# Second product of a two-layer network: two of its three partial products take bfloat16 operands

## The chip, the cores and the metric

The kernel runs on one core of one Trainium2 chip. The metric is the device time of one execution in microseconds (us). The kernel before was timed three times: median 1087.86 us, from 1087.34 to 1088.19.

## The reference, cut to what matters

```python
# attention with exponential features: 8 batches x 8 heads, 576 tokens, 64 wide, 128 features
def phi(x):
    proj = x @ w_phi
    proj = proj - max(abs(proj), axis=-1)
    return concatenate([exp(proj), exp(-proj)])
kv, z = phi(k).T @ v, sum(phi(k), tokens)
x = (phi(q) @ kv) / (phi(q) @ z + 1e-06)     # gathered to [4608 tokens, 512]

# then the two-layer network
h = x @ w_in                                  # 512 -> 2048
g = maximum(h, 0.0) ** 2
out = g @ w_out                               # 2048 -> 512
```

All inputs and outputs are float32.

## The kernel before, in words

The program has two parts that run interleaved. The attention part works on 32 pairs of heads (four pairs make a batch). It writes its result, split into two float16 arrays (a rounded value and the rest), into a ring buffer in SBUF that holds 1536 tokens. The network part reads that ring.

The network part cuts the 4608 tokens into 18 chunks of 256 and the 2048 hidden columns into 8 slices of 256. Function `moe(c, f, ...)` handles one chunk and one slice, so there are 144 steps. One step is:

1. `gemm1` (TensorE, line 934) forms the hidden slice in a PSUM tile `ph` of 128 x 512 words. `w_in` and the ring are both kept as two float16 parts, and three of the four part products are formed: 24 matmuls, each with 128 x 128 weights and 256 moving columns.
2. ScalarE takes the relu with a scale (line 943, tile `r`), squares it into `gh` (line 945), rounded to float32r, and squares it again at full precision into PSUM (line 952; in the first 16 steps VectorE does that instead).
3. VectorE subtracts (helper at line 288): `gl` is the exact square less `gh`, and is written as float32r, a four-byte word like `gh`.
4. `gemm2` (TensorE, line 962) adds the slice's share to two output tiles `po` in PSUM, one for each 128 tokens (`i`), 512 columns each. `w_out` is kept as `wout[f][0]` (rounded to float32r) and `wout[f][1]` (the rest, also in float32r). For each `i` and each 128 hidden columns (`j`) it multiplies `gh` by `wout[f][0]`, `gh` by `wout[f][1]` and `gl` by `wout[f][0]`: 12 matmuls of 512 moving columns. The activations are the stationary operand, the weights the moving one.
5. After slice 7 of a chunk, VectorE scales `po` into the tile `o` (line 973), of which there is one buffer, and SyncE's queue stores it (line 976). This is done for `i` = 0 and then for `i` = 1.

The order of instructions on each engine is fixed when the program is built. Every piece of work is registered with an engine, a duration, what it needs and which buffers it uses (`P.add`). A list scheduler (`order`) simulates the engines by these durations. `improve` repeats that 400 times, moves the ranks of a twentieth of the early pieces at random each time, and keeps the shortest plan. So a changed duration of one kind of work can give another order everywhere, in the start of the program too, where SyncE's loads, the attention of the first pairs and the preparation of the weights compete.

Of the kernel before, what the change touches and what calls it, by code (L numbers as in the profile page):

```python
# [15 lines left out]
F32R = mybir.dt.float32r  # L16
F16 = mybir.dt.float16
BF16 = mybir.dt.bfloat16
# [17 lines left out]
T = 256  # L36
# [217 lines left out]
def act_us(n, pointers=0):  # L254
    return 0.2 + n / 1200 + 0.09 * pointers
# [19 lines left out]
def tile_kernel(ctx, tc, qp, kp, vp, w_phi, w_in, w_out, out):  # L275
    nc = tc.nc
    V, A, G, PE, SP = nc.vector, nc.scalar, nc.gpsimd, nc.tensor, nc.sync
    P = Plan()
# [3 lines left out]
    mp = ctx.enter_context(tc.tile_pool(name="moe", bufs=1))  # L282
# [4 lines left out]
    def sub(eng, out_, a, b_):  # L287
        eng.tensor_tensor(out=out_, in0=a, in1=b_, op=ALU.subtract)  # L288

    def tiles(pool, tag, shape, dtype, bufs, first=0):  # L290
        return Tiles(P, pool, tag, shape, dtype, bufs, first)
# [8 lines left out]
    wout = [None] * NFP  # L300
# [43 lines left out]
    po_ = tiles(ps, "po", [128, DM], F32, 2)  # L344

    r_ = tiles(mp, "r", [128, 2, T], F32, 2)
    gh_ = tiles(mp, "gh", [128, 2, T], F32R, 3)
    gl_ = tiles(mp, "gl", [128, 2, T], F32R, 3)
    o_ = tiles(mp, "o", [128, DM], F32, 1)

    dq = cp.tile([32, 2, 32], F32, name="dq")
# [564 lines left out]
    def moe(c, f, w_done):  # L916
        n = c * NFP + f
        m, bank = LEAD + n, n + 2 * BANKS
        half, c0 = divmod(c * T % RING, HR)
        po = [("po", 2 * BANKS + 2 * c + i) for i in range(2)]  # L920

        after = list(w_done[f, True])
        if f == 0:
            for p in range(NPAIR):
                after += [o for t0, t1, o in ring_of[p] if t0 < c * T + T and t1 > c * T]

        def gemm1():
            ph = ph_[bank]
            for j in range(2):
                ff = 2 * f + j  # L930
                k = 0
                for t in range(KT):
                    for (w, x) in ((0, 0), (0, 1), (1, 0)):
                        PE.matmul(out=ph[:, j, :], lhsT=win[w][:, t, 128 * ff:128 * ff + 128],  # L934
                                  rhs=ring[half][x][:, t, c0:c0 + T], start=k == 0, stop=k == 3 * KT - 1)
                        k += 1

        g1 = P.add("PE", 2.58, gemm1, after, [("ph", bank)], m)
        if f:
            g1.after.append(chunk_done[c][-1])  # L940
        chunk_done.setdefault(c, []).append(g1)
        Q = m - 1000.0
        o = P.add("ACT", act_us(512, 1), lambda: A.activation(  # L943
            out=r_[n], in_=ph_[bank], func=AF.Relu, scale=cw[:, f, 0:1]), [g1], [("ph", bank), ("r", n)], Q)
        sq = P.add("ACT", act_us(512), lambda: A.activation(out=gh_[n], in_=r_[n], func=AF.Square),  # L945
                   [o], [("r", n), ("gh", n)], Q)
        if n < WITH_DVE:
            o = P.add("DVE", 0.76, lambda: V.scalar_tensor_tensor(
                out=ph_[bank], in0=ph_[bank], scalar=cw[:, f, 0:1], in1=r_[n], op0=ALU.mult, op1=ALU.mult),
                [o], [("ph", bank), ("r", n)], Q)  # L950
        else:
            o = P.add("ACT", act_us(512), lambda: A.activation(out=ph_[bank], in_=r_[n], func=AF.Square),  # L952
                      [sq], [("ph", bank), ("r", n)], Q)
        o = P.add("DVE", 0.70, lambda: sub(V, gl_[n], ph_[bank], gh_[n].bitcast(F32)),
                  [o, sq], [("ph", bank), ("gh", n), ("gl", n)], Q)

        def gemm2():
            for i in range(2):
                for j in range(2):
                    ff = 2 * f + j  # L960
                    for s, (g, w) in enumerate(((gh_, 0), (gh_, 1), (gl_, 0))):
                        PE.matmul(out=po_[po[i][1]], lhsT=g[n][:, j, 128 * i:128 * i + 128], rhs=wout[f][w][:, j, :],  # L962
                                  start=(ff == 0 and s == 0), stop=(ff == 2 * NFP - 1 and s == 2))

        g2 = P.add("PE", 2.86, gemm2, [o] + list(w_done[f, False]),
                   [("gh", n), ("gl", n)] + po, m + 1.5)
        if f:
            g2.after.append(last2[0])
        last2[0] = g2
        if f == NFP - 1:  # L970
            for i in range(2):
                tt = 2 * c + i
                o = P.add("DVE", 0.8, lambda tt=tt, i=i: V.tensor_scalar(
                    out=o_[tt], in0=po_[po[i][1]], scalar1=cc[:, tt:tt + 1], scalar2=cc[:, tt:tt + 1],
                    op0=ALU.mult, op1=ALU.mult), [g2], [po[i], ("o", tt)], Q)
                P.add("SP", 0.1, lambda tt=tt: SP.dma_start(out[128 * tt:128 * tt + 128, :], o_[tt]),
                      [o], [("o", tt)], Q, land=2.5)
# [5 lines left out]
    w_done = {}  # L983
# [33 lines left out]
    for c in range(NCH):  # L1017
        for f in range(NFP):
            moe(c, f, w_done)
# [37 lines left out]
```

## Time and profile before

| what | value |
|---|---|
| time, median of 3 runs | 1087.86 us |
| time of the profiled execution | 1087.31 us |
| its span, first to last instruction | 1085.5 us |
| TensorE matmuls (PE) | 1063.7 us busy, 98% of the span, 7882 matmuls |
| TensorE weight loads (PEld) | 826.3 us busy, 76% |
| VectorE (DVE) | 737.3 us busy, 68% |
| ScalarE (ACT) | 632.9 us busy, 58% |
| GpSimd (POOL) | 185.6 us busy, 17% |
| mean granted TensorE clock | 0.997 of full speed |

The profile is of one execution. Matmuls are pipelined, so the busy time of one matmul in it (390 ns, say) is longer than the distance to the next one. What a matmul costs in a dense stretch is read from the distance between starts, or from the chain of waits, which gives the length of whole blocks of matmuls. In that chain "PE po L962 x12" is one `gemm2` and "PE ph L934 x24" one `gemm1`.

### The profile page before, as it was taken

The numbers are of one execution on the slowest core, as the hardware profiler recorded it, in microseconds if no ns is written. First come the engines' busy times: TensorE is split into PE (matmuls) and PEld (weight loads), VectorE is DVE, ScalarE is ACT, GpSimd is POOL, SyncE is SP. The second block draws the span as 40 slices with busy tenths as digits, with TensorE's granted clock in tenths as the row PEclk, the third lists the DMA queues.
The fourth block names the chain that finished last, engine by engine and source line by source line (L and its number), as shares of the span: only waits on it lengthen the run. The fifth ranks groups of instructions, "written<-read, shape, count | busy, mean of one in ns | idle before, by whom it ended". The sixth has DMA issues, their size and how long they took to land.

```text
span 1085.5 us, 19971 instructions
## 1 busy us (share of the span) xinstructions
PE 1063.7 (98%) x7882; PEld 826.3 (76%) x7882; DVE 737.3 (68%) x1537; ACT 632.9 (58%) x1125; POOL 185.6 (17%) x87
## 2 busy tenths in 40 slices
PE   7889999999999999999999999999999999999997
PEld 6656777777777777777777777877777777888886
DVE  4589989787778877877878776776777855112111
ACT  6889864466566665656556655665555645333232
POOL 1366531111111111111111111111100111000000
PEclk9999999999999999999999999999999999999999
DMA  8844412212212122222222111112120101000000
GB/s 304 309 126 117 149 46 68 59 35 56 85 45 85 46 75 55 69 62 57 74 56 75 55 60 38 54 55 75 43 63 22 50 14 41 1 21 20 1 20 20
DMA packets 68288, 73.49 MB, mean 68 GB/s; under 512 B 36836, under 2 KB 41828, under 8 KB 68196
## 3 DMA queue, kind: packets, MB, share of 16 engines
q1 hardware_dynamic: 68196, 72.23, 21.8%
q8 instruction: 62, 1.02, 0.4%
q14 instruction: 30, 0.25, 0.1%
HBM read 59.18 MB, written 12.99 MB: 66 GB/s over the span
## 4 chain that ended last, share of the span: by engine, by line
PE 88%; DVE 4%; ACT 3%; DMA 2%; issue 1%; POOL 1%; SPq 0%; DVEq 0%; POOLq 0%
PE po L962 35%; PE ph L934 33%; PE pv L568 4%; PE pp L512 3%; PE pn L786 3%; PE pp L855 3%; PE pv L786 2%; PE pv L573 1%; PE pp L665 1%; PE pn L518 1%; DVE u L415 1%; DMA k<-in_kp_dram 1%; DMA den<-sx 1%; ACT u L412 1%; POOL u L426 1%
## 5 line engine op out<-in xcount | busy, mean ns | idle before, releaser
L934 PE MATMUL ph<-ring,win 128*128 128x256 f16 x3456 | 399.4, 273 | 0.1
L934 PEld LDWEIGHTS <-win 128*128 128x128 f16 x3456 | 328.2, 98 | 67.9 <-issue 30.2
L962 PE MATMUL po<-wout,gh 128*128 128x512 f32 x1152 | 369.6, 402 | 0.0
L962 PEld LDWEIGHTS po<-wout,gh 128*128 128x128 f32 x1152 | 206.8, 189 | 47.8 <-issue 5.6
L943 ACT ACTIVATE r<-ph,cw 128x512 f32<-128x512 f32 x144 | 98.8, 686 | 234.1 <-PE ph L934 233.9
L962 PE MATMUL po<-wout,gl 128*128 128x512 f32 x576 | 226.3, 393 | 0.0
L868 POOL PARTITION_ALL_REDUCE mx<-pt x52 | 113.6, 2184 | 634.3 <-ACT pt L862 528.3
L288 DVE TENSOR_TENSOR gl<-ph,gh 128x512 fp32r<-128x512 f32 x144 | 98.7, 686 | 166.1 <-ACT ph L952 163.5
L962 PEld LDWEIGHTS po<-wout,gl 128*128 128x128 f32 x576 | 108.1, 188 | 25.1 <-DVE gl L288 0.5
L945 ACT ACTIVATE gh<-r 128x512 fp32r<-128x512 f32 x144 | 90.9, 631 | 4.6
L952 ACT ACTIVATE ph<-r 128x512 f32<-128x512 f32 x128 | 74.7, 583 | 0.0
L808 ACT ACTIVATE n<-pn 128x320 f32<-128x320 f32 x26 | 11.4, 438 | 102.4 <-PE pn L786 102.4
L568 PE MATMUL pv<-e,v 128*64 128x256 f32 x512 | 60.9, 380 | 0.4 <-ACT kz L615 0.4
L882 DVE SCALAR_TENSOR_TENSOR pt<-qe,zc,pt 128x576 f32<-128x576 f32 x52 | 42.2, 813 | 22.4 <-ACT pt L880 21.4
L288 DVE TENSOR_TENSOR qe<-pt,mx 128x576 f32<-128x576 f32 x52 | 39.2, 754 | 22.6 <-POOL mx L868 22.3
L534 ACT ACTIVATE e<-e 128x512 f32<-128x512 f32 x64 | 39.8, 621 | 21.4 <-DVE e L531 21.2
L568 PEld LDWEIGHTS pv<-e,v 128*64 128x64 f32 x512 | 35.5, 137 | 15.1 <-ACT kz L615 0.5
L873 ACT ACTIVATE qe<-qe 128x576 f32<-128x576 f32 x52 | 35.0, 673 | 17.2 <-DVE qe L288 17.1
L819 DVE STREAM_TRANSPOSE kvs<-pv 128x256 f32<-128x256 f32 x26 | 11.6, 445 | 47.7 <-PE pv L786 44.4
L880 ACT ACTIVATE pt<-qe,zc 128x576 f32<-128x576 f32 x52 | 39.6, 771 | 3.3
L886 DVE STREAM_TRANSPOSE yt<-pt 128x576 f32<-128x576 f32 x52 | 40.4, 776 | 1.3
L536 ACT ACTIVATE e<-e 128x512 f32<-128x512 f32 x64 | 40.2, 629 | 1.7
(196 smaller groups left out, 1296.0 us busy)
## 6 DMA issues: line engine op xcount, KB each, us to landing
v<-in_vp_dram SPq DMA_DIRECT2D x32, 320.0 KB
k<-in_kp_dram SPq DMA_DIRECT2D x32, 288.0 KB
q<-in_qp_dram SPq DMA_DIRECT2D x32, 288.0 KB
rb<-rd SPq DMA_DIRECT2D x64, 144.0 KB
out_dram<-o SPq DMA_DIRECT2D x36, 256.0 KB
td<-kvs SPq DMA_DIRECT2D x26, 128.0 KB
kz<-td SPq DMA_DIRECT2D x208, 16.0 KB
raw0i<-in_w_in_dram SPq DMA_DIRECT2D x1, 1024.0 KB
```

The lines of the kernel that those rows point to most:

```text
L288: eng.tensor_tensor(out=out_, in0=a, in1=b_, op=ALU.subtract)
L536: exps[p].append(P.add("ACT", act_us(512), lambda n=n: A.activation(out=e_[n][:, :, 0, :], in_=e_[n][:, :, 0, :], func=AF.Exp), [o], [("e" ...
L568: PE.matmul(out=to[64 * h:64 * h + 64, 0:256], lhsT=v_[p][:, t, h, :], rhs=e_[2 * p + h][:, t].rearrange("p s f -> p (s f)"), start=t == 0 ...
L786: PE.matmul(out=to[64 * h:64 * h + 64, :], lhsT=kz_[n][:, 128 * s_ + 64 * h:128 * s_ + 64 * h + 64], rhs=qe_[2 * n + h].rearrange("p (s x) ...
L868: o = P.add("POOL", par_us(S), lambda n=n, h=h: G.partition_all_reduce(mx_[n], pt_[p][:, h, :], channels=128, reduce_op=bass_isa.ReduceOp. ...
L882: o = P.add("DVE", dve_us(S), lambda h=h, qe=qe, y=y: V.scalar_tensor_tensor(out=y(), in0=qe(1), scalar=zc_[p][:, 2 * h + 1:2 * h + 2], in ...
L886: o = P.add("DVE", dve_us(S), lambda n=n, y=y: V.transpose(yt_["y", n - 2 * EARLY], y()), [o], [("pt", p), ("yt", ("y", n - 2 * EARLY))], ...
L934: PE.matmul(out=ph[:, j, :], lhsT=win[w][:, t, 128 * ff:128 * ff + 128], rhs=ring[half][x][:, t, c0:c0 + T], start=k == 0, stop=k == 3 * K ...
L943: o = P.add("ACT", act_us(512, 1), lambda: A.activation(out=r_[n], in_=ph_[bank], func=AF.Relu, scale=cw[:, f, 0:1]), [g1], [("ph", bank), ...
L945: sq = P.add("ACT", act_us(512), lambda: A.activation(out=gh_[n], in_=r_[n], func=AF.Square), [o], [("r", n), ("gh", n)], Q)
L952: o = P.add("ACT", act_us(512), lambda: A.activation(out=ph_[bank], in_=r_[n], func=AF.Square), [sq], [("ph", bank), ("r", n)], Q)
L962: PE.matmul(out=po_[po[i][1]], lhsT=g[n][:, j, 128 * i:128 * i + 128], rhs=wout[f][w][:, j, :], start=(ff == 0 and s == 0), stop=(ff == 2 ...
```

## The change

`gl` becomes a bfloat16 tile. Two of the three partial products in `gemm2` take bfloat16 operands: the product of `gh` and the rest of the weights, and the product of `gl` and the rounded weights. Where a float32r tile is an operand there, only the upper two bytes of each word are read, through a bfloat16 view with a step of two elements. This is so for the stationary `gh` in the second product and for the moving weights in both. The stationary `gl` is contiguous. The product of `gh` and `wout[f][0]` stays in float32r. The loop over the three products becomes the outermost one, and the duration that the scheduler is told for a `gemm2` goes from 2.86 to 2.72.

```diff
-    gl_ = tiles(mp, "gl", [128, 2, T], F32R, 3)
+    gl_ = tiles(mp, "gl", [128, 2, T], BF16, 3)
...
         def gemm2():
-            for i in range(2):
-                for j in range(2):
-                    ff = 2 * f + j
-                    for s, (g, w) in enumerate(((gh_, 0), (gh_, 1), (gl_, 0))):
-                        PE.matmul(out=po_[po[i][1]], lhsT=g[n][:, j, 128 * i:128 * i + 128], rhs=wout[f][w][:, j, :],
+            upper = lambda x: x.bitcast(BF16).rearrange("p j (c w) -> p j c w", w=2)[:, :, :, 1]
+            for s, (g, w) in enumerate(((gh_[n], wout[f][0]), (upper(gh_[n]), upper(wout[f][1])),
+                                        (gl_[n], upper(wout[f][0])))):
+                for i in range(2):
+                    for j in range(2):
+                        ff = 2 * f + j
+                        PE.matmul(out=po_[po[i][1]], lhsT=g[:, j, 128 * i:128 * i + 128], rhs=w[:, j, :],
                                   start=(ff == 0 and s == 0), stop=(ff == 2 * NFP - 1 and s == 2))

-        g2 = P.add("PE", 2.86, gemm2, [o] + list(w_done[f, False]),
+        g2 = P.add("PE", 2.72, gemm2, [o] + list(w_done[f, False]),
```

The order of instructions moves in the whole program. Two places of it matter below. The first is TensorE at the very end, the last `gemm2` of the program (`po_11598` is the output tile of `i` = 0, `po_11605` and in the changed kernel `po_11601` that of `i` = 1; `gh_11846` and `gl_11849` are its activations). Before:

```order
L962 MATMUL po_11598<-wout_1731,gh_11846 128x512 x2
L962 MATMUL po_11598<-wout_1731,gl_11849 128x512
L962 MATMUL po_11598<-wout_1731,gh_11846 128x512 x2
L962 MATMUL po_11598<-wout_1731,gl_11849 128x512
L962 MATMUL po_11605<-wout_1731,gh_11846 128x512 x2
L962 MATMUL po_11605<-wout_1731,gl_11849 128x512
```

And in the changed kernel:

```order
L965 MATMUL po_11598<-wout_1659,gh_11846 128x512 x2
L965 MATMUL po_11601<-wout_1659,gh_11846 128x512 x2
L965 LDWEIGHTS gh_11846
L965 MATMUL po_11598<-wout_1659,gh_11846 128x512
...
L965 LDWEIGHTS gl_11849
L965 MATMUL po_11598<-wout_1659,gl_11849 128x512
L965 LDWEIGHTS gl_11849
L965 MATMUL po_11598<-wout_1659,gl_11849 128x512
L965 LDWEIGHTS gl_11849
L965 MATMUL po_11601<-wout_1659,gl_11849 128x512
```

Before, the tile of `i` = 0 had all its shares after six of the twelve matmuls; now it has them after ten. A bfloat16 matmul has a weight load of its own in the program, as the float16 ones of `gemm1` have; a float32r matmul is one instruction that loads its own weights.

The second place is the queue of loads on SyncE at the start of the program (`k`, `q` and `v` are a pair's inputs, `raw0i` and `raw1i` the first two slices of `w_in`; the difference, with - for before and + for the changed kernel):

```order
 L504 DMA k_116<-in_kp_dram 128x576
 L505 DMA q_118<-in_qp_dram 128x576
 L469 DMA v_120<-in_vp_dram 128x640
+L403 DMA raw1i<-in_w_in_dram 128x4x512
+L504 DMA k_158<-in_kp_dram 128x576
+L505 DMA q_162<-in_qp_dram 128x576
+L469 DMA v_167<-in_vp_dram 128x640
 L403 DMA raw0i<-in_w_in_dram 128x4x512
-L469 DMA v_149<-in_vp_dram 128x640
-L504 DMA k_159<-in_kp_dram 128x576
-L505 DMA q_164<-in_qp_dram 128x576
```

One slice of `w_in` stands ahead of the second pair's keys in both, the other slice now and `raw0i` before; the second pair's `v` is now behind its keys and queries.

## Prediction

> **What bounds the kernel now.** I read the page's first and fourth parts first, then busy time by stretches, then who waited for whom.
>
> ```profile
> span 1085.5 us, 19971 instructions
> PE 1063.7 (98%) x7882; PEld 826.3 (76%) x7882; DVE 737.3 (68%) x1537; ACT 632.9 (58%) x1125; POOL 185.6 (17%) x87
> PE 88%; DVE 4%; ACT 3%; DMA 2%; issue 1%; POOL 1%; SPq 0%; DVEq 0%; POOLq 0%
> PE po L962 35%; PE ph L934 33%; PE pv L568 4%; PE pp L512 3%; PE pn L786 3%; PE pp L855 3%; PE pv L786 2%; PE pv L573 1%; PE pp L665 1%; PE pn L518 1%; DVE u L415 1%; DMA k<-in_kp_dram 1%; DMA den<-sx 1%; ACT u L412 1%; POOL u L426 1%
> 0.00:120.00 120.00, 104.24 (x1054) 73.59 (x1055) 87.20 (x142) 100.86 (x168) 54.10 (x28) 0.99 0.60 205
> 120.00:1080.00 960.00, 959.42 (x6831) 752.71 (x6828) 649.33 (x1395) 532.04 (x958) 131.51 (x59) 1.00 0.18 50
> PE pn L375 <- DVE et L541: 0.3, 1, 0.3
> ```
>
> The last three are the two stretches (length, then busy us of PE, PEld, DVE, ACT, POOL, then granted clock) and the whole list of TensorE's waits after 120 us: one wait, 0.3 us. From 120 to 1080 us TensorE is busy 959.42 of 960 us at clock 1.00. So a nanosecond taken off a matmul there comes off the end, and `gemm2` is 35% of the chain. TensorE idles only at the start, 120 − 104.24 = 15.8 us, and after its last matmul.
>
> What a matmul costs is read from the chain of waits in a dense late stretch (start, length, block) and from the groups:
>
> ```profile
> 950.45 2.76 PE po L962 x12
> 953.21 5.26 PE ph L934 x48
> 958.47 5.48 PE po L962 x24
> L934 PE MATMUL ph<-ring,win 128*128 128x256 f16 x3456 | 399.4, 273 | 0.1
> L934 PEld LDWEIGHTS <-win 128*128 128x128 f16 x3456 | 328.2, 98 | 67.9 <-issue 30.2
> L962 PE MATMUL po<-wout,gh 128*128 128x512 f32 x1152 | 369.6, 402 | 0.0
> L962 PEld LDWEIGHTS po<-wout,gh 128*128 128x128 f32 x1152 | 206.8, 189 | 47.8 <-issue 5.6
> L962 PE MATMUL po<-wout,gl 128*128 128x512 f32 x576 | 226.3, 393 | 0.0
> ```
>
> A float32r matmul of 512 columns takes 2.76 / 12 = 230 ns (228 in the block of 24). A float16 one of 256 columns takes 5.26 / 48 = 109.6 ns; two of them, 512 columns, take 219 ns. So columns of two-byte operands already go by at a higher rate here, with their weight load (98 ns) under the 109.6 ns. The 189 ns load of a float32r matmul lies under 230 ns.
>
> **The change part by part.**
>
> *Eight of twelve matmuls, in 144 steps: 1152 matmuls.* Each took 230 ns. A contiguous two-byte matmul of 512 columns isn't in the trace. It is bounded above by the two halves, 219 ns, since these hold whatever fixed part a matmul has twice. The fixed part is at most what the 109.6 ns leave beside the 98 ns load, some 11 ns, so the lower bound is 219 − 11 = 208 ns. I take 216, a fixed part of 3 ns, nearer to the upper bound because nothing suggests that a load sets the pace at 256 columns. The saving is 14 ns each (11 to 22), so 1152 × 14 ns = 16.1 us (12.7 to 25.3).
>
> [...]
>
> *The step of two.* No two-byte operand with a step is in the trace. The nearest row for the moving side is the float32r matmul itself: a step of two over two-byte elements passes over the same 2 KB per partition and product as the 512 four-byte words, which go by in 230 ns. So the memory delivers those bytes at least at that rate, and the bound above is no gain at all (230, the first rival). Below it is the contiguous 216. I take 216: in the profile nothing separates bytes passed over from bytes used. On the stationary side (`gh`, 576 loads) the bounds are the 98 ns and 189 ns loads. Either fits under a 216 ns matmul.
>
> [...]
>
> *The change of type within a step.* After a float32r matmul, the next float16 load isn't drawn under it:
>
> ```profile
> 952.82 0.39 PE L962 MATMUL po<-wout,gl 128*128 128x512 f32 x1
> 953.05 5.42 PE L934 MATMUL ph<-ring,win 128*128 128x256 f16 x48
> 953.05 0.44 PEld L934 LDWEIGHTS <-win 128*128 128x128 f16 x5 [0.26 <-issue]
> ```
>
> The loads stand idle 0.26 us until the float32r matmul has run its 0.23 us. The cost is small: the 48 that follow keep to 109.6 ns on average. This switch moves from the end of `gemm2` to its middle, and the one from two-byte to four-byte operands stays at the start. I take 0. If the strided load that now stands there were slow, 189 − 98 = 91 ns more in each step would be uncovered, 144 × 91 ns = 13.1 us (second rival).
>
> *What stays.* 576 float32r matmuls at 230 ns. VectorE's subtraction writes two bytes instead of four:
>
> ```profile
> L288 DVE TENSOR_TENSOR gl<-ph,gh x144: 640/691/694, 106.8 to 1076.4; 128x512 fp32r<-128x512 f32 x144
>   PEld po L962: 0.5, 1
>   PEld L934: 0.4, 1
> ```
>
> The last two rows are TensorE's only waits for it, 0.9 us in all. `gl` is now needed at the ninth matmul, not the third, some 1.3 us later. Its cover is the steps between `gemm1` and `gemm2` in TensorE's order: 0, even if the subtraction's 691 ns should change either way by a third (0.23 us).
>
> *The end.* The last `gemm2`, VectorE's scaling and the stores (SPq: SyncE's queue):
>
> ```profile
> 1077.07 0.62 PE L962 MATMUL po<-wout,gh 128*128 128x512 f32 x2
> 1078.63 0.81 DVE L973 TENSOR_SCALAR o<-po,cc 128x512 f32<-128x512 f32 x1 [1.56 <-PE po L962]
> 1079.47 3.30 SPq L976 DMA_DIRECT2D out_dram<-o  x2
> 1079.57 0.39 PE L962 MATMUL po<-wout,gl 128*128 128x512 f32 x1
> 1081.60 0.81 DVE L973 TENSOR_SCALAR o<-po,cc 128x512 f32<-128x512 f32 x1 [2.16 <-DMA out_dram<-o]
> ```
>
> The second scaling at 1081.60 waits for the first store, because `o` has one buffer, and not for TensorE, which started its last matmul 2 us earlier. So the end hangs on the moment when the tile of `i` = 0 is complete. That was after 6 matmuls, 6 × 0.230 = 1.38 us from the block's start; now it is after ten, 4 × 0.230 + 6 × 0.216 = 2.22 us. That adds 0.8 us. The other tile is complete two matmuls later and still waits for the store. At the other 17 chunk ends TensorE has `gemm1` blocks to do: 0 there.
>
> *The order.* The scheduler's other order changes the start. Of the 15.8 us idle before 120 us, the wait for the first keys stays:
>
> ```profile
> PE po L512 <- DMA k<-in_kp_dram: 4.9, 2, 4.6
> ```
>
> The other 11 us hang on which of many short waits come last. In both orders a slice of `w_in` precedes the second pair's keys. I have no row for the new order and take 0, within ±3 us (a quarter of what is open).
>
> **Sum:** 1087.31 (the profiled execution) − 16.1 + 0.8 = 1072.0 us. The median before lies 0.55 above that execution, so I predict 1072.5 us. The likeliest case's own range is 1062 to 1079: the saving's bounds and ±3 for the start.
>
> **Rivals.**
>
> 1. *A strided word costs what a float32r word costs.* If the 14 ns come from passing 2 KB per partition through the port, they stay, as all eight matmuls have a strided moving operand. For it: the only matmuls here with four bytes per column are the ones at 230. Against it: nothing in the rows, for there is no second length of float32r to tell a fixed part from a rate. Time: 1087.86 + 0.8 = 1088.7, within ±3.
> 2. *The late load is slow.* In each step the strided load after the last float32r matmul stands open for 91 ns more: 1072.5 + 13.1 = 1085.6. If it isn't overlapped with the next load either, 2 × 13.1 brings 1098.7. For it: the 0.26 us gap shows that this load isn't drawn forward. Against: the five loads after the gap, 98 ns each, end within 0.44 us, less than 5 × 98 = 490 ns, so one of them ran beside another.
> 3. *Slower: the moving port halves its rate at a step of two*, two reads where one served. Place: every one of the 1152. Price: 432 ns instead of 216, so 1152 × (432 − 230) ns = 232.7 us, 1321 us. It decides as soon as a strided column costs over 6.5% (14 of 216 ns) more than a contiguous one: then the gain is gone and every further per cent is 2.5 us of loss. For it: no such operand has a row. Against: a four-byte column already takes only 230.
> 4. *The new start loses what TensorE wins.* It would take twice the 11 us that are open there. Little speaks for it.
>
> **How the numbers follow.** The forecast gets 0.76, rival 1 0.10, rival 2 0.07, rival 3 0.03, rival 4 and the rest 0.04. A measurement of this kernel can tell about 0.2% (2.2 us) from no change. Faster than 1085.7 is the forecast whole, half of rival 2 and a part of the rest: 0.81. Within 0.2%: most of rival 1 at 1086 to 1090 and a part of rival 2: 0.09. Slower: rival 3, the long form of rival 2, the upper part of rival 1: 0.10. The range is 1064 to 1085.6: it holds nearly all of the forecast's own and the short form of rival 2, and leaves out 2 in 10.
>
> **What would show it.** In the changed profile a whole `gemm2` should be 4 × 230 + 8 × 216 = 2.65 us in the chain of waits (2.76 before), and its bfloat16 loads should take 98 ns. 2.76 would be rival 1. A gap of over 0.1 us between the fourth and the sixth matmul of a block would be rival 2. A block over 4 us would be rival 3. After 120 us TensorE should still wait for almost nothing, and its idle time before 120 us should be 13 to 19 us. The second scaling at the end should start about 2.97 us after the first, and that 2.2 us into the last block. The forecast is wrong if the blocks are shorter but TensorE waits in the middle, or if bfloat16 with a step keeps 230.

## The result and the profile after

The changed kernel takes 1095.68 us (median of 14 runs, 1093.43 to 1097.23), the kernel before 1087.78 us in the same comparison. The ratio is 1.0064, with a 95% interval from 1.005 to 1.0078: slower, by 7.9 us, where 1072.5 us was forecast. The profiled execution took 1096.09 us.

The page of the changed kernel: its span, the busy time, the granted clock in 40 slices, and the groups of the second product.

```profile
span 1094.3 us, 19959 instructions
PE 1065.5 (97%) x7882; PEld 719.7 (66%) x7882; DVE 739.7 (68%) x1537; ACT 634.6 (58%) x1125; POOL 181.6 (17%) x87
PEclk9898899999999999999999999999999999999999
L965 PE MATMUL po<-wout,gl 128*128 128x512 bf16 x576 | 153.2, 387 | 0.0
L965 PEld LDWEIGHTS <-gl 128*128 128x128 bf16 x576 | 55.1, 96 | 74.7
L965 PEld LDWEIGHTS <-gh 128*128 128x128 bf16 x576 | 44.5, 98 | 76.3 <-issue 39.3
```

The kernel does what the change says (the clock's row is read further down): all 1152 matmuls are bfloat16 and their weight loads take 96 to 98 ns instead of 188. Two things differ from the forecast. The first is the length of a block in the chain of waits (start, length, block):

```profile
953.71 2.75 PE po L965 x12
961.82 5.24 PE ph L934 x48
967.06 5.49 PE po L965 x24
```

A `gemm2` takes 2.75 us. It was 2.76 before and was forecast at 2.65. The second is the start. Here are the first 120 us as a whole, then cut in two places (length, busy us of PE, PEld, DVE, ACT and POOL, granted clock, share and rate of the DMAs), and TensorE's longest waits:

```profile
0.00:120.00 120.00, 98.82 (x972) 67.62 (x973) 83.88 (x137) 98.11 (x162) 47.19 (x27) 0.90 0.60 205
...
40.00:60.00 20.00, 15.46 (x157) 10.61 (x158) 10.40 (x22) 13.83 (x26) 6.33 (x4) 0.83 0.54 184
100.00:120.00 20.00, 15.78 (x130) 9.17 (x130) 17.28 (x23) 17.88 (x28) 11.65 (x6) 0.74 0.41 124
...
PE pp L656 <- ACT qe L674: 5.7, 3, 4.5
PE pn L518 <- DMA k<-in_kp_dram: 4.2, 1, 4.2
PE po L512 <- DMA k<-in_kp_dram: 2.3, 1, 2.3
```

By 120 us TensorE has finished 972 matmuls, against 1054 before, and its clock is granted at 0.90, against 0.99. In the clock's row above, the slices with an 8 are the second, the fourth and the fifth, all within the first 137 us. The network part starts later. This is the group of the relu, which every step has once (duration, then first and last start), before and after:

```profile
L943 ACT ACTIVATE r<-ph,cw x144: 662/687/700, 103.5 to 1074.5; 128x512 f32<-128x512 f32 x144
```

```profile
L943 ACT ACTIVATE r<-ph,cw x144: 666/688/706, 123.9 to 1082.5; 128x512 f32<-128x512 f32 x144
```

The 8.8 us between the two profiled spans (1085.5 and 1094.3) fall into three parts, by the times in the traces. The 21st relu starts at 251.0 us before and at 263.3 us after: 12.3 us lost. From there to the last relu it takes 823.5 us before and 819.3 after: 4.2 us won. From the last relu to the end it takes 11.0 and 11.7 us: 0.7 us lost. (These times, and others to the nanosecond below, are starts read from the traces at full resolution.)

The end is as forecast. The last block, the scalings and the stores of the changed kernel:

```profile
1087.59 0.81 DVE L976 TENSOR_SCALAR o<-po,cc 128x512 f32<-128x512 f32 x1 [2.48 <-PE po L965]
1088.42 3.29 SPq L979 DMA_DIRECT2D out_dram<-o  x2
1090.55 0.81 DVE L976 TENSOR_SCALAR o<-po,cc 128x512 f32<-128x512 f32 x1 [2.15 <-DMA out_dram<-o]
```

The first scaling starts 5.1 us after the last relu (1082.5), 4.1 us before.

So two questions had to be settled: why the bfloat16 matmuls won so little, and whether the start lost its time through the order of instructions.

### The profile page after: what moved, and what is told of

It reads as the page before. It is cut to its first block, busy times and chain, and to the rows that moved or that the text cites. A ratio compares the mean times of both kernels' runs of the same rounds, so it can differ in the third digit from the quotient of the medians.

```text
span 1094.3 us, 19959 instructions
## 1 busy us (share of the span) xinstructions
PE 1065.5 (97%) x7882; PEld 719.7 (66%) x7882; DVE 739.7 (68%) x1537; ACT 634.6 (58%) x1125; POOL 181.6 (17%) x87
## 4 chain that ended last, share of the span: by engine, by line
PE 91%; ACT 2%; DVE 1%; DMA 1%; issue 1%; DVEq 0%; ACTq 0%
PE po L965 37%; PE ph L934 35%; PE pv L568 4%; PE pp L512 3%; PE pn L786 3%; PE pp L855 2%; PE pv L786 2%; PE pv L573 1%; PE pp L665 1%; PE pn L518 1%; DMA raw5o<-in_w_out_dram 0%; PE pn L682 0%; ACT u L412 0%; PE pp L656 0%; DVE u L415 0%
## 5 line engine op out<-in xcount | busy, mean ns | idle before, releaser
L934 PEld LDWEIGHTS <-win 128*128 128x128 f16 x3456 | 335.8, 98 | 72.4 <-issue 6.4
L965 PE MATMUL po<-wout,gh 128*128 128x512 f32 (+1 forms) x1152 | 302.9, 404 | 0.0
L288 DVE TENSOR_TENSOR gl<-ph,gh 128x512 bf16<-128x512 f32 x144 | 98.6, 685 | 168.1 <-ACT ph L952 165.1
L965 PE MATMUL po<-wout,gl 128*128 128x512 bf16 x576 | 153.2, 387 | 0.0
L965 PEld LDWEIGHTS po<-wout,gh 128*128 128x128 f32 x576 | 98.1, 189 | 23.8 <-issue 3.8
L965 PEld LDWEIGHTS <-gl 128*128 128x128 bf16 x576 | 55.1, 96 | 74.7
L965 PEld LDWEIGHTS <-gh 128*128 128x128 bf16 x576 | 44.5, 98 | 76.3 <-issue 39.3
L534 ACT ACTIVATE e<-e 128x512 f32<-128x512 f32 x64 | 39.7, 621 | 22.4 <-DVE e L531 22.4
```

The costliest lines, as they stand in the source:

```text
L965: PE.matmul(out=po_[po[i][1]], lhsT=g[:, j, 128 * i:128 * i + 128], rhs=w[:, j, :], start=(ff == 0 and s == 0), stop=(ff == 2 * NFP - 1 an ...
```

## Experiments

### Order and product apart

The duration that the scheduler is told was set back, so that every engine has the order of before, with the changed product:

```diff
-        g2 = P.add("PE", 2.72, gemm2, [o] + list(w_done[f, False]),
+        g2 = P.add("PE", 2.86, gemm2, [o] + list(w_done[f, False]),
```

> The changed second product, but with the duration 2.86 told to the scheduler, so that every engine has the order of the kernel before. Theory A (the new order of the start lost about 15 us, the matmuls won about 6): clock mean 1.00 and about 1054 matmuls in the first 120 us, as before; time 1087.8 - 6.5 + 0.8 = 1082. Rival B (the bfloat16 products are themselves what lost the time): about 1095, as the changed kernel.

And the reverse, the product of before (all float32r) with the duration 2.72, so in the order of the changed kernel:

```diff
-        g2 = P.add("PE", 2.86, gemm2, [o] + list(w_done[f, False]),
+        g2 = P.add("PE", 2.72, gemm2, [o] + list(w_done[f, False]),
```

> The second product of before, all in float32r, but with the duration 2.72, so that every engine has the order of the changed kernel. Theory A: about 1101 (1087.8 and some 14 us lost in the first 120 us, with a mean clock of about 0.90 there). Rival B: about 1088, no change.

In the order of before, the changed product takes 1086.94 us (1082.25 to 1093.24), ratio 1.0002 (0.9983 to 1.0022): no difference that can be measured. The order alone takes 1097.73 us, ratio 1.0091 (1.0073 to 1.0108). The first 120 us of the two, in the columns used above:

```profile
0.00:120.00 120.00, 104.97 (x1071) 73.32 (x1074) 88.29 (x147) 102.74 (x172) 55.70 (x29) 0.97 0.63 210
```

```profile
0.00:120.00 120.00, 98.64 (x968) 66.87 (x968) 88.58 (x137) 97.93 (x161) 48.88 (x27) 0.91 0.61 205
```

1071 matmuls with the order of before, 968 with the other, whatever the product is. The product of before in the new order loses the start as the changed kernel does: its 21st relu starts at 263.5 us. So the whole loss is the order's, and theory A holds in kind. Its numbers don't: it had 1082 and 1101, and 1086.94 and 1097.73 were measured (the profiled execution of order_of_before, 1083.68 us, is one of its faster ones). The product's gain is smaller than theory A had it. With equal orders, 123 steps from the 21st relu to the last take 823.5 us with float32r and 821.0 us with the change, and in the other order 822.1 and 819.3 us. That is 20 to 23 ns a step, where 112 ns were forecast.

### The step of two

The next kernel, in the order of before, reads the same number of two-byte elements of the same tiles, but neighbouring ones, so its output isn't the reference's. All further kernels of this section have the order of before too.

```diff
-            for s, (g, w) in enumerate(((gh_[n], wout[f][0]), (upper(gh_[n]), upper(wout[f][1])),
-                                        (gl_[n], upper(wout[f][0])))):
+            first = lambda x: x.bitcast(BF16)[:, :, 0:512]
+            for s, (g, w) in enumerate(((gh_[n], wout[f][0]), (upper(gh_[n]), first(wout[f][1])),
+                                        (gl_[n], first(wout[f][0])))):
```

> As order_of_before, but the moving operand of the eight bfloat16 matmuls is 512 neighbouring two-byte elements of the same weights instead of every second one; the output is therefore not the reference's, the count and sizes of the matmuls stay. Theory C (the step of two costs some 10 ns in 512 columns): 216 ns a matmul instead of 226, 1152 x 10 ns = 11.5 us below order_of_before, about 1070. Rival D (226 ns is what 512 two-byte columns take): the same time as order_of_before, 1082.

It takes 1074.83 us, ratio 0.989 (0.9873 to 0.9908). The stationary `gh` still has its step of two there. The distance between starts is read from the last product of a step, four matmuls with `gl`, to the first matmul of the next `gemm1`. First the changed kernel, then this one:

```profile
960.75 1.06 PE L965 MATMUL po<-wout,gl 128*128 128x512 bf16 x4
961.66 0.81 PE L934 MATMUL ph<-ring,win 128*128 128x256 f16 x6
```

```profile
960.47 1.03 PE L966 MATMUL po<-wout,gl 128*128 128x512 bf16 x4
961.33 2.78 PE L934 MATMUL ph<-ring,win 128*128 128x256 f16 x24
```

The distances are 0.91 / 4 and 0.86 / 4 us. At the trace's full resolution the medians are 225.5 ns with a step and 216 ns without. The forecast's 216 is right for neighbouring elements, and the step of the moving operand costs the 10 ns that theory C has, though the time is 1074.83 where theory C had about 1070. The steps from the 21st relu to the last took 811.8 us, 74 ns a step less than with the step of two: 8 × 9.3 ns.

Two further kernels ask whether that is a price per matmul or per byte. One cuts nearly all matmuls of the product in two:

```diff
-                        PE.matmul(out=po_[po[i][1]], lhsT=g[:, j, 128 * i:128 * i + 128], rhs=w[:, j, :],
-                                  start=(ff == 0 and s == 0), stop=(ff == 2 * NFP - 1 and s == 2))
+                        cuts = (0, 512) if ff == 0 and s == 0 else (0, 256, 512)
+                        for lo_, hi_ in zip(cuts, cuts[1:]):
+                            PE.matmul(out=po_[po[i][1]][:, lo_:hi_], lhsT=g[:, j, 128 * i:128 * i + 128],
+                                      rhs=w[:, j, lo_:hi_], ...)
```

> As order_of_before, but nearly all matmuls of the second product are cut into two of 256 columns (all but the first product of slice 0's first half); only the distance between starts is read. Theory 'rate' (a strided or four-byte column is slower by a fixed share): a strided half takes 113 ns, half of 225.5, and a float32r half 113 to 115. Theory 'fixed part' (each such matmul has 10 to 13 ns on top): strided halves 117 to 119 ns, float32r halves 117 to 120 ns. Contiguous float16 at 256 columns is 109 ns.

The other takes wider steps over more of the weights' memory:

```diff
-    (upper(gh_[n]), upper(wout[f][1])), (gl_[n], upper(wout[f][0]))
+    (upper(gh_[n]), wout[f][1].bitcast(BF16).rearrange("p j (c w) -> p (j c) w", w=4)[:, :, 3]),
+    (gl_[n], wout[f][2].bitcast(BF16).rearrange("p i j (c w) -> p (i j c) w", w=8)[:, :, 7])
```

> As order_of_before, but the moving operand of the correction with gh takes every fourth, and that of the correction with gl every eighth two-byte element of the weights' memory (512 of them each, other values than the reference's); only the distance between starts is read. If the cost goes with the bytes passed over (2 KB cost 10 ns): 235 and 255 ns. If only a step as such costs: 226 and 226 ns. If each new piece of memory must be opened for one element: up to 430 ns at step 8. [...]

The halves, eight matmuls of 256 columns with `gl`:

```profile
962.62 1.07 PE L967 MATMUL po<-wout,gl 128*128 128x256 bf16 x8
963.52 2.67 PE L934 MATMUL ph<-ring,win 128*128 128x256 f16 x23
```

0.90 / 8 = 113 ns, half of 225.5: the theory of a rate. At these two lengths a strided column costs a fixed share more, and no extra part for each matmul shows. Float32r halves took 119 ns, over half of their 227 to 230, which is the range of the other theory: two halves take 238 ns, 8 to 11 ns more than one whole, so float32r seems to have a fixed part of that size (an estimate from these two lengths). The wide steps, every fourth element with `gh` and every eighth with `gl`:

```profile
1502.39 1.54 PE L965 MATMUL po<-wout,gh 128*128 128x512 bf16 x3 [0.28 <-issue]
1503.74 3.78 PE L965 MATMUL po<-wout,gl 128*128 128x512 bf16 x4
1507.34 4.06 PE L934 MATMUL ph<-ring,win 128*128 128x256 f16 x24
```

1.35 / 3 = 450 ns at step 4 and 3.60 / 4 = 900 ns at step 8 (medians 453 and 900). A matmul passes over 2 KB of each partition at step 2, 4 KB at step 4 and 8 KB at step 8, and takes 226, 453 and 900 ns. With a step the time goes with the bytes passed over, used or not, 2 KB in 225 ns. Without a step 1 KB takes 216 ns, where 256 columns at step 2 pass over 1 KB in 113 ns, so there the bytes alone don't set the time. The granted clock tells the two apart as well. It was at half in many stretches of this kernel, and there the float16 matmuls of `gemm1` went from 109 to 213 ns apart, while those with steps 4 and 8 stayed at 453 and 900: TensorE's clock doesn't set their pace. None of the three expected values for steps 4 and 8 was met: the price is linear in the bytes, but all of the time is price, not the 10 ns alone. A float32r matmul of 512 columns passes the same 2 KB and takes 227 to 230 ns, so reading half of each word left little to win. Whether the same limit sets the pace of float32r isn't shown; its halves, at 119 ns and not 113, say that something comes on top.

So for TensorE's moving operand a step costs 4% more time at two elements, 2.1 times the time at four and 4.2 times at eight (225.5, 453 and 900 ns against 216). The stationary operand was tried at a step of two alone: the strided loads of `gh` take 98 ns, the contiguous ones of `gl` 96 ns, and both are shorter than the 225.5 ns of a matmul.

### The two tiles one after the other

```diff
-            for s, (g, w) in enumerate(...):
-                for i in range(2):
+            for i in range(2):
+                for s, (g, w) in enumerate(...):
                     for j in range(2):
```

> As order_of_before, but the loop over the two output tiles is outermost, so that the first tile is complete after six matmuls again; each block then has two changes from float32r to bfloat16 and back instead of one. Theory E (the end hangs on the first tile, a change of type costs nothing): 0.8 us below order_of_before. Rival F (a change of type costs 10 to 20 ns): 144 x 10 to 20 ns more, 0.6 to 2.1 us above it.

It takes 1088.03 us, ratio 1.0016 (1.0 to 1.0032); beside the 1.0002 (0.9983 to 1.0022) of order_of_before that is no clear difference, so the traces have to tell. In the trace, the first scaling comes 4.2 us after the last relu instead of 5.0 us: theory E's 0.8 us, and the end does hang on the first tile. But the last 33 steps take 186.0 us instead of 185.2 us: 26 ns a step for one more change from float32r to bfloat16 and back (20 ns over the 123 steps used above). So a change of type isn't free, which is rival F at or somewhat above its 10 to 20 ns. The weight loads of the order_of_before kernel show where it arises:

```profile
956.82 0.88 PEld L965 LDWEIGHTS po<-wout,gh 128*128 128x128 f32 x4
957.96 0.57 PEld L965 LDWEIGHTS <-gh 128*128 128x128 bf16 x4 [0.27 <-issue]
958.66 0.77 PEld L965 LDWEIGHTS <-gl 128*128 128x128 bf16 x4
```

The first bfloat16 load after the float32r ones waits 0.27 us, until the running matmul is through. The kernel before has the same gap, 0.26 us, at the end of its `gemm2`. So where `gemm1` and `gemm2` alternate, the changed kernel changes type as often as before, and there the step went from 5.400 to some 5.367 us: 33 ns won (47 of the 123 steps; measured against order_alone, which has the float32r product in the same order), near 8 × (230 − 225.5) = 36 ns. Where two `gemm2` stand in a row, a long run of float32r is now broken once more: the block of 24 takes 5.49 us, against 5.48 before, and these 13 steps won 3 ns each. The other 63 won 19 ns each; why less than 33 was not taken apart.

### Why the start is slow

The changed kernel's longest wait stands at 42.7 to 47.2 us: `PE pp L656 <- ACT qe L674`, 4.5 us. ScalarE stands still for 5.5 us there, because its next instruction overwrites the scratch tile `sx`, which a small store of denominators still reads: it was issued at 36.9 us behind two 1 MB loads of weights, and what waits for it goes on at 43.9. (The clock is halved from 45.9 to 52.7 us in this trace, later than the expectation below has it.) The experiment gives that instruction a tile of its own, in the order of the changed kernel:

```diff
-                out=sx_["va", p].bitcast(BF16)[:, 0:640], in_=v_[p].rearrange("p t h d -> p (t h d)"), func=AF.Abs,
+                out=sva, in_=v_[p].rearrange("p t h d -> p (t h d)"), func=AF.Abs,
```

> The changed kernel in its own order, but the scan for the largest value of v (ScalarE, the 640-wide write into sx) writes into a tile of its own. In the changed kernel that write waits 5.5 us at 38.5 us for the small store of the denominators to leave sx, and TensorE waits 4.54 us behind it with the clock halved from 37.5 to 44.4 us. Theory G (this one wait, with the halved clock around it, is a large part of the 12 us lost at the start): that wait is gone, the half-clock time near 40 us is gone or shorter, 1089 to 1092. Rival H (other waits end last there): 1094 to 1096, no change.

It takes 1093.37 us (1092.4 to 1098.6), ratio 1.0067 (1.0046 to 1.0089), where the changed kernel has 1.0064 (1.005 to 1.0078). The wait is gone, but no time is won that the ratios show. TensorE's waits in this kernel, and its first 120 us:

```profile
PE pn L519 <- DMA k<-in_kp_dram: 5.4, 1, 5.4
PE pn L683 <- ACT sx L707: 2.5, 1, 2.5
...
PE pp L657 <- ACT qe L675: 1.2, 2, 0.8
```

```profile
0.00:120.00 120.00, 99.89 (x952) 67.50 (x953) 85.68 (x135) 96.47 (x158) 47.05 (x26) 0.90 0.61 204
```

The wait for `qe` fell from 5.7 to 1.2 us. Others took its place, and the clock is still 0.90. This execution is the slowest of the six, 1098.6 us at a mean clock of 0.987; four took 1092.4 to 1093.6 us at 0.991 to 0.994. The median lies between the ranges of theory G (1089 to 1092) and rival H (1094 to 1096), so a gain of 1 or 2 us isn't excluded. A large part of the 12 us this wait was not, so theory G falls. Other single waits were not tested.

Is 2.72 a bad value, or is every order a draw of the random search? Three kernels with other seeds answer that: 2.72 with seed 2, 2.86 with seed 2, and 2.72 with seed 3, all with the changed product.

```diff
-TRIALS, SEED, MOVED = 400, 1, 70.0
+TRIALS, SEED, MOVED = 400, 2, 70.0
```

> The changed kernel with another seed (2) of the scheduler's random moves. Theory A (the start is a draw of the search, and the draw of the changed kernel was a poor one): another time than 1095.7 by several us, anywhere from 1083 to 1100, and it follows TensorE's waits and the half-clock time of the first 120 us. Rival (any order planned with 2.72 starts badly): 1094 to 1097 again.

> The changed product with the scheduler's duration at 2.86 again and the other seed (2). Theory A (the start is a draw, and the order of before a good one): it starts late as other_draw did, the first step's relu after 108 us, 1092 to 1100. Rival (2.72 itself makes bad starts): first relu at 101 to 104 us as in the kernel before, 1083 to 1087.

> The changed kernel (2.72) with a third seed (3). Theory A: another time again, between 1083 and 1100. Rival: 1094 to 1100, as the two draws with 2.72 so far.

| order (with the changed product) | time, us | ratio to before | TensorE's waits to 126 us | half clock, to 130 us | 21st relu |
|---|---|---|---|---|---|
| 2.86, seed 1: order_of_before | 1086.94 | 1.0002 (0.9983 to 1.0022) | 14.8 | 6.8 | 248.9 |
| 2.86, seed 2: other_draw_286 | 1092.78 | 1.0049 (1.0031 to 1.0067) | 20.3 | 17.1 | 260.1 |
| 2.72, seed 1: the changed kernel | 1095.68 | 1.0064 (1.005 to 1.0078) | 22.5 | 23.9 | 263.3 |
| 2.72, seed 2: other_draw | 1100.51 | 1.011 (1.0067 to 1.0152) | 24.0 | 10.2 | 263.0 |
| 2.72, seed 3: third_draw | 1105.25 | 1.0163 (1.0139 to 1.0188) | 27.6 | 34.1 | 263.7 |

(Waits, half-clock time and relu are those of one profiled execution each, in us; the times of the last two are medians of two runs, that of other_draw_286 of three.) With 2.86 a different seed starts late too, so 2.72 is not needed for a late start. That it adds something isn't excluded: its three orders are the three slowest of five, and the last, at 1105.25 us, lies above both ranges that were expected. Five orders of one program spread over 18 us, and the order of before is the best of them. It stands in the time of the kernel before as a lucky draw, and a changed duration can draw again. The last row also has more attention work late: its 41st relu starts at 415.0 us, against 406.7 us in the changed kernel.

How the loss divides into waiting and slow clock can't be read cleanly: both fall into the same stretch, and no run shows which brings the other. One program shows how time goes with the clock: the 12 runs of order_of_before lie around a line of 0.8 us for each 0.001 of mean clock (1082.25 us at 0.996, 1093.24 us at 0.990). Against the profiled execution of that kernel, the changed one has 17 us more at half clock, which is 0.008 of its mean clock and would be some 6 us by this line. Its waits are 7.7 us longer, and its 21st relu starts 14.3 us later. This division is an estimate and was not tested by itself: no kernel held the clock up while the waits stayed.

### A version that is faster than both

The weights of the two corrections are kept a second time as contiguous bfloat16 tiles, in the order of before.

```diff
+                packed = cp.tile([128, 2, 2, DM], BF16, name=f"packed{f}", tag=f"wb{f}")
+                wout[f] = [cp.tile([128, 2, DM], F32R, name=f"wout{f}", tag=f"wa{f}"), packed[:, 0], packed[:, 1]]
                 A.activation(out=wout[f][0], in_=value(2), func=AF.Copy)
+                V.tensor_copy(out=wout[f][2], in_=value(2))
...
-            (upper(gh_[n]), upper(wout[f][1])), (gl_[n], upper(wout[f][0]))
+            (upper(gh_[n]), wout[f][1]), (gl_[n], wout[f][2])
```

> As order_of_before, with the two corrections' weights kept a second time as contiguous bfloat16 arrays, so that no moving operand has a step; the raw weights are loaded and prepared in two halves to make room, and VectorE makes one more copy for each of the eight slices of w_out. Theory C (the step costs 9 to 10 ns in a matmul): blocks as in contiguous_moving, 1075 us, plus up to 4 us that the extra instructions cost at the start: 1075 to 1079. Rival (the speed of contiguous_moving came from the values it read): 1084 to 1088.

It takes 1080.74 us, ratio 0.9936 (0.9911 to 0.9961), above the 1075 to 1079 that were expected. The steps run as in contiguous_moving (811.2 us from the 21st relu to the last), with the right weights, so the values that contiguous_moving read were not what made it fast. But the start is later, 255.9 us at the 21st relu against 248.9 in the profiled execution of order_of_before, more than the 4 us allowed for the preparation in halves. A part of that may be the clock, with 10.2 us at half speed against 6.8. With the separate scratch tile and the first output tile completed first in the very last block:

```diff
+            turns = [(s, x, i) for s, x in products for i in range(2)]
+            if c == NCH - 1 and f == NFP - 1:
+                turns.sort(key=lambda y: y[2])
```

> packed_weights with the separate scratch tile, and with the first output tile completed first in the very last block alone. Theory: 0.8 us less at the end (the second scaling starts 2.1 us instead of 2.9 us after the last block is two thirds done), and no change from the scratch tile, since the order of before doesn't wait there: 1079.9 against 1080.7 of packed_weights. If the scratch tile helps this order too: 1076 to 1079.

This takes 1079.36 us, ratio 0.9931 (0.9914 to 0.9948), the fastest full version here. Its first scaling starts 4.0 us after the last relu instead of 4.9 us, which is the 0.9 us of the end; the rest of the difference is within the spread of the runs.

## Why the prediction was wrong, point by point

*TensorE sets the time after 120 us, so that a nanosecond off a matmul comes off the end.* Right: its only wait there after the change is 1.3 us at 121 us, and the 4.2 us saved per matmul and by the order came off the middle part.

*1152 matmuls at 216 ns, 16.1 us.* Wrong in one step. 216 is what a contiguous bfloat16 matmul takes (216 measured). The failing step is "The step of two": both ends stood there, 230 with the memory's rate as the limit and 216 without, and the end without was taken "since nothing separates bytes passed over from bytes used". They are not separate: 225.5 ns measured, set by the 2 KB passed over, as the kernels with steps 4 and 8 and with halves show. Rival 1 named that mechanism and had a chance of 0.10. The reason given for it, that the only matmuls with four bytes per column are the slow ones, was the row that should have weighed more. The rest of the term was sound: with packed weights, so without the step, 123 steps take 811.2 us instead of 823.5, 100 ns a step of the 112 forecast.

*The change of type at 0.* Right where `gemm1` and `gemm2` alternate, since the change only moves there. Missed where two `gemm2` stand in a row: there the changed kernel has one change more, and one more change measured 20 to 26 ns a step, at the late load that the prediction quoted. That is 0.2 to 0.3 of the 91 ns of rival 2, whose mechanism (a slow strided load) didn't occur: 98 ns.

*The end, 0.8 us.* Right: the first scaling starts 0.9 us later after the last relu, and the second still waits for the store by the one buffer that the prediction named.

*VectorE's subtraction at 0.* Right: 692 ns after (median), 691 before, and TensorE's weight loads wait for it for 0.4 us in all.

*The order at 0, within ±3 us.* The step that decided the sign. 12.3 us were lost, and TensorE's idle time before 120 us was 21.2 us, where 13 to 19 were expected. The ±3 was "a quarter of what is open", and what was open counted only waiting, not the clock; and it took the order of before for a typical one. Rival 4 had the place and the size (11 us) and almost no chance; it counted waits alone.

The middle of the forecast fell by the product's price (about 13 of 16 us), and its sign by the order. The forecast's own range has a slip in its sum: with a saving of 25.3 us and 3 us less at the start its lower end is 1060, not 1062.

## What to carry to other kernels

A two-byte view with a step over four-byte data made TensorE's moving operand hardly cheaper here (225.5 ns against 227 to 230): count the bytes that the view passes over, 2 KB per partition in 225 ns, and pack the moving operand where the gain is wanted (216 ns); the stationary one may keep a step of two (98 ns a load against 96). Where a scheduler with a random search orders the program, compare a change at an unchanged order first, and take the spread of other seeds (18 us here) as the uncertainty of any change that touches a duration.

## What was not expected of the hardware

The time of a strided moving operand went with the bytes passed over: 226, 453 and 900 ns for 512 bfloat16 columns at steps 2, 4 and 8, 113 ns for 256 columns at step 2. Without a step 512 columns took 216 ns.

Where the granted clock is at half, matmuls with steps 4 and 8 keep their 453 and 900 ns, while float16 ones in the same kernel go from 109 to 213 ns.

The granted clock falls to half in parts of these starts, in which TensorE is 77 to 88% busy (92.1 to 106.1 of 120 us): the stretches are 3.4, 6.8, 10.2 and 13.7 us long, all multiples of 3.4 us. The profiled execution of tile_by_tile, at 86%, has none in its start. What halves the clock was not shown. Waits alone don't account for it: in the kernel with steps 4 and 8 the mean clock was 0.856 although TensorE waited only some 34 us after the first 126 of 1786 us. That was seen in this one kernel only.
